# Sliding-window attention with a mixture of adapters: q and k in 16-row runs, v as fp32 with a cast on GpSimd, contiguous score columns, and a list-scheduled emission

## The chip, the cores and the metric

The kernel runs on one core of a Trainium2 chip. The metric is the time of one execution on the device in microseconds (us); lower is better. Times "before" are of the kernel as it stood, "after" of the changed one.

## The reference

```python
def _attn_ref(q, k, v):                  # q, k, v: (8, 8, 576, 64) = batch, head, position, d
    window = 32
    scores = (1.0 / np.sqrt(D)) * np.matmul(q, k.transpose(0, 1, 3, 2))
    mask = np.abs(pos[:, None] - pos[None, :]) <= window
    scores = np.where(mask, scores, -1000000000.0)
    attn = np.exp(scores - np.max(scores, axis=-1, keepdims=True))
    attn = attn / (np.sum(attn, axis=-1, keepdims=True) + 1e-09)
    return np.matmul(attn, v)

def _moe_ref(x, w_gate, A, B):           # x: (4608, 512), 8 adapters of rank 16
    logits = x @ w_gate                  # the two largest logits of a row choose two adapters
    # w = softmax over these two; delta = sum over the two of w * ((x @ A[e]) @ B[e])
    return (x + delta).astype(np.float32)

x = attn_out.transpose(0, 2, 1, 3).reshape(B * S, H * D)   # heads side by side
```

## The kernel before

**Units.** Two heads of a batch make a pair; 8 batches of 4 pairs give 32 units. A unit has 9 blocks of 64 keys; a block meets the 128 queries around it. Two heads stand in one matmul: kT holds the pair's keys as a block-diagonal 128 x 128 weight, so the 128 score rows are 64 keys of each head. The 288 blocks are taken 8 at a time: 36 score tiles.

**Stages.** `load` (L75) brings q and k of a batch with a cast to fp16, three DMAs of 96 partitions each for q and three for k, in runs of two rows (512 bytes read, 256 written). `load_v` (L86) brings v of a batch with a cast, straight into `vbd`, in 16 DMAs of 288 runs each (256 bytes read, 128 written). All of them are issued by GpSimd (POOL). `pair_heads` (L92, VectorE) puts the heads of a pair side by side, `transposes` (L167) turns them on TensorE, and `qTs`, `kTs` receive them (L171 and L176 on VectorE, L177 on ScalarE). `score` adds the mask by a matmul with the identity (L182, two of 512 columns per tile), then one matmul of 128 columns per block (L186); its result is written with a step of two columns in PSUM. ScalarE takes the exponential (L191) into one of four `PTs`. `pv` (L206) is 13 matmuls of 130 columns per unit, and VectorE normalises (L214, L215) into `xs`.

**Adapters.** Per batch `moe_step` transposes xs (L227, copied by L230), multiplies by A and w_gate (`moe_zl`, L238), runs a chain of small VectorE operations for the gate (L248 to L262, with one exponential on ScalarE, L254), transposes the result (L271, copied by ScalarE L274) and forms B's part plus xs (L282, L284), which ScalarE copies out (L287) and SP stores (L291).

**Order.** The program emits unit by unit: transposes two units ahead, scores one unit ahead, `pv` of the unit, then a quarter of the previous batch's `moe_step`. PSUM tiles come from a pool of three of 4 KB per partition (`pw`) and one of two of 2 KB (`pt`). Each engine runs its instructions in the order in which they stand. A DMA that POOL issues waits, besides what its data asks for, on the semaphore of the eighth POOL DMA before it, since eight such semaphores are used in turn; DMAs of SP have eight of their own.

**Start.** POOL issues q and k of batch 0, makes `ident`, issues v of batch 0, and makes `mask`.

Of the kernel before, what the change touches and what calls it, by code (L numbers as in the profile page):

```python
# [21 lines left out]

@with_exitstack
def kernel(
# [37 lines left out]

    NV = 3
    vbd = [const.tile([128, NP, NB, 2 * VD], F16, name=f"vbd{i}") for i in range(NV)]

    def load(b, w):
        d = load_pool.tile([96, 3, H, 2, D], F16, tag=f"l{w}", name=f"l{w}")
        src = (q, k)[w][b].rearrange("h (g p j) d -> g p h (j d)", g=3, j=2)
        for g in range(3):
            nc.gpsimd.dma_start(  # L75
                out=d[:, g].rearrange("p h j d -> p h (j d)"), in_=src[g])
        raw[b, w] = d

    def load_v(b):
        d = vbd[b % NV]  # L80
        src = v[b].rearrange("(n h) (a p j) d -> h j n p a d", h=2, p=32, j=2)
        for n in range(NP):
            for h in range(2):
                for j in range(2):
                    p0 = 64 * h + 32 * j
                    nc.gpsimd.dma_start(  # L86
                        out=d[p0:p0 + 32, n, :, VD * h:VD * h + D], in_=src[h, j, n])

    def pair_heads(b, w):
        d = cast_pool.tile([96, 3, 2, H, D], F16, tag=f"c{w}", name=f"c{w}")  # L90
        for g in range(3):
            nc.vector.tensor_copy(out=d[:, g],  # L92
                                  in_=raw[b, w][:, g].rearrange("p h j d -> p j h d"))
        qk[b, w] = d

    raw, qk = {}, {}
    load(0, 0)
    load(0, 1)

    ident = const.tile([128, 128], F16)  # L100
    make_identity(nc, ident)

    for i in range(NV):
        nc.vector.memset(vbd[i], 0.0)
        nc.vector.memset(vbd[i][0:64, :, :, D], 1.0)
        nc.vector.memset(vbd[i][64:128, :, :, VD + D], 1.0)

    load_v(0)
    pair_heads(0, 0)
    pair_heads(0, 1)  # L110


    mask = const.tile([128, 4, 128], F16)
    nc.gpsimd.memset(mask, 0.0)
    for s in range(4):
        jk = s % 2
        blk = mask[32 * s:32 * s + 32]
        nc.gpsimd.affine_select(out=blk, in_=blk, compare_op=ALU.is_ge, fill=NEG,
                                base=-jk, channel_multiplier=-2,
                                pattern=[[0, 4], [1, 128]])  # L120
        nc.gpsimd.affine_select(out=blk, in_=blk, compare_op=ALU.is_ge, fill=NEG,  # L121
                                base=64 + jk, channel_multiplier=2,
                                pattern=[[0, 4], [-1, 128]])

    NQ = 4
    qTs = [const.tile([128, 2, 320], F16, name=f"qT{i}") for i in range(NQ)]
    kTs = [const.tile([128, NB, 128], F16, name=f"kT{i}") for i in range(NQ)]
    for t in qTs:
        nc.vector.memset(t[:, :, 0:16], 0.0)
# [245 lines left out]
```

## Time and profile before

| | us |
|---|---|
| median of 2 runs | 216.5 (215.47 and 217.53) |
| span of the profiled execution | 211.4 |
| from the start to the first `pv` matmul | 34.3 |
| from there to the last `pv` | 159.5 |
| from there to the end | 17.6 |

The page gives the profiled execution by its span, from the first to the last instruction; 216.5 stands 5.1 us above it. Durations below come from this one execution. PE is TensorE's matmuls, PEld its weight loads, DVE VectorE, ACT ScalarE, POOL GpSimd, SP the engine that issues the stores. A run of matmuls is pipelined: the mean of one (some 220 ns for 128 columns) is not its price in a stream, which is read from the chain of waits, where a run of n matmuls stands with its share of the time.

### The profile page before, as it was taken

The page shows a single profiled execution, that of the slowest core. Times are in us where ns is not written, and L with a number is a line of the kernel's source. Part 1 is how long each engine was busy: PE and PEld are TensorE (multiplying, and loading weights), DVE is VectorE, ACT ScalarE, POOL GpSimd, SP SyncE. Part 2 cuts the span into 40 slices and gives each one's busy share as a digit, 9 for nine tenths or more (in the row PEclk, how much of TensorE's full clock was granted, in tenths as well). Part 3 has the DMA queues.
Part 4 walks back from the last instruction along what each step waited for, and adds up shares of the span by engine and source line. Part 5 has one row for each costly group of instructions (what it writes and reads, how often), then busy time and mean ns, then how long its engine had stood idle before and what let it go on. Part 6 is the DMA issues. An engine that isn't in the chain of part 4 may idle for free.

```text
span 211.4 us, 4124 instructions
## 1 busy us (share of the span) xinstructions
PE 147.6 (70%) x1600; PEld 114.4 (54%) x1600; DVE 119.9 (57%) x337; ACT 85.6 (40%) x109; POOL 128.3 (61%) x197
## 2 busy tenths in 40 slices
PE   0030279998299949987699729964998599848481
PEld 0010158996268835876378626864687468726330
DVE  6787026668814891379346851688349734844700
ACT  2001015663357334553275144723683466246032
POOL 7999995999799469835983797699480000000000
PEclk9999999999969995999699997999999999999955
DMA  6998099999999998998999999999993023003306
GB/s 59 157 63 56 1 140 125 67 42 154 138 101 144 244 96 54 208 210 87 63 167 249 103 89 153 258 98 147 172 189 55 0 90 136 5 0 123 100 0 223
DMA packets 86642, 24.12 MB, mean 114 GB/s; under 512 B 81888, under 2 KB 82016, under 8 KB 86624
## 3 DMA queue, kind: packets, MB, share of 16 engines
q0 software_dynamic: 81376, 14.44, 86.3%
q1 hardware_dynamic: 5248, 9.44, 13.2%
q8 instruction: 12, 0.20, 0.4%
q14 instruction: 6, 0.05, 0.1%
HBM read 28.85 MB, written 9.44 MB: 181 GB/s over the span
## 4 chain that ended last, share of the span: by engine, by line
PE 52%; DVE 19%; POOL 11%; ACT 9%; issue 4%; DMA 3%; ACTq 0%; POOLq 0%
PE ps L186 13%; PE po L206 9%; PE ps L182 7%; PE pd L282 5%; PE tp L167 5%; PE pd L284 5%; POOL vbd_82 L86 4%; DVE xb L215 4%; PE pz L238 3%; DMA l_189<-in_k_dram 3%; DVE zs L262 3%; PE tx L227 3%; DVE xT L230 3%; ACT zT L274 3%; PE tz L271 2%
## 5 line engine op out<-in xcount | busy, mean ns | idle before, releaser
L86 POOL DMA_DIRECT2D vbd_83<-in_v_dram x48 | 29.3, 616 | 12.0 <-DMA vbd_83<-in_v_dram 4.8
L86 POOL DMA_DIRECT2D vbd_82<-in_v_dram x48 | 29.3, 617 | 9.0 <-DMA l_496<-in_q_dram 2.7
L182 PE MATMUL ps<-mask,ident 128*128 128x512 f16 x72 | 24.6, 423 | 12.7 <-POOL mask L121 12.0
L214 DVE RECIPROCAL rc<-po 128x10 f32<-128x10 f32 x32 | 7.0, 218 | 38.2 <-PE po L206 38.1
L287 ACT COPY obt<-pd 128x1024 f32<-128x1024 f32 (+1 forms) x24 | 20.8, 869 | 16.8 <-PE pd L284 16.0
L215 DVE TENSOR_TENSOR xb<-po,rc 128x640 f16<-128x640 f32 x32 | 26.2, 820 | 0.7
L86 POOL DMA_DIRECT2D vbd_84<-in_v_dram x32 | 19.5, 619 | 7.3 <-DMA vbd_84<-in_v_dram 2.6
L282 PE MATMUL pd<-B_sb,zT 128*128 128x512 f16 x40 | 18.3, 459 | 4.2 <-ACT zT L274 4.2
L271 PE MATMUL tz<-ident,zs 128*128 128x128 f16 x40 | 4.0, 234 | 21.0 <-DVE zs L262 21.0
L227 PE MATMUL tx<-ident,xb 128*128 128x128 f16 x160 | 14.7, 220 | 5.4 <-DVE xT L230 4.8
L284 PE MATMUL pd<-xb,ident 128*128 128x512 f16 x40 | 18.4, 461 | 0.0
L230 DVE COPY xT<-tx 128x512 f16<-128x512 f16 x40 | 15.6, 416 | 2.4 <-PE tx L227 1.6
L177 ACT COPY kT_164<-tp 64x576 f16<-64x576 f16 x8 | 5.1, 633 | 25.0 <-DVE kT_164 L176 25.0
L227 PEld LDWEIGHTS <-xb 128*128 128x128 f16 x160 | 11.3, 101 | 6.9 <-issue 4.9
L271 PEld LDWEIGHTS <-zs 128*128 128x128 f16 x40 | 2.4, 102 | 22.8 <-DVE zs L262 22.8
L182 PEld LDWEIGHTS <-ident 128*128 128x128 f16 x72 | 6.6, 110 | 14.3 <-issue 14.1
L238 PE MATMUL pz<-WA_sb,xT 128*128 128x136 f16 x160 | 13.9, 223 | 0.4 <-DVE xT L230 0.4
L186 PE MATMUL ps<-qT_160,kT_164 128*128 128x128 f16 x72 | 11.1, 317 | 2.4 <-ACT kT_164 L177 2.4
L177 ACT COPY kT_161<-tp 64x576 f16<-64x576 f16 x8 | 5.1, 634 | 18.2 <-DVE kT_161 L176 18.1
L274 ACT COPY zT<-tz 128x640 f16<-128x640 f16 x8 | 5.5, 692 | 16.6 <-PE tz L271 16.6
L191 ACT ACTIVATE PT_178<-ps 128x1024 f16<-128x1024 f32 x9 | 9.2, 1023 | 6.6 <-PE ps L186 5.7
L191 ACT ACTIVATE PT_180<-ps 128x1024 f16<-128x1024 f32 x9 | 9.2, 1023 | 6.1 <-PE ps L186 5.2
(209 smaller groups left out, 375.4 us busy)
## 6 DMA issues: line engine op xcount, KB each, us to landing
out_dram<-obt SPq DMA_DIRECT2D x24, 256.0 KB, 4.0
out_dram<-obt SPq DMA_DIRECT2D x16, 192.0 KB, 2.7
vbd_82<-in_v_dram POOLq DMA_DIRECT2D x48, 36.0 KB, 2.8
vbd_83<-in_v_dram POOLq DMA_DIRECT2D x48, 36.0 KB, 3.4
vbd_84<-in_v_dram POOLq DMA_DIRECT2D x32, 36.0 KB, 3.2
l_85<-in_q_dram POOLq DMA_DIRECT2D x3, 192.0 KB, 4.8
l_89<-in_k_dram POOLq DMA_DIRECT2D x3, 192.0 KB, 6.4
l_185<-in_q_dram POOLq DMA_DIRECT2D x3, 192.0 KB, 4.6
```

What stands on the lines that cost most here:

```text
L86: nc.gpsimd.dma_start(out=d[p0:p0 + 32, n, :, VD * h:VD * h + D], in_=src[h, j, n])
L182: nc.tensor.matmul(out=ps[:, i:i + 4], lhsT=ident, rhs=mask, start=True, stop=False)
L186: nc.tensor.matmul(out=ps[:, i].rearrange("p (k j) -> p j k", j=2), lhsT=kTs[u % NQ][:, a, :], rhs=qTs[u % NQ][:, :, 32 * a:32 * a + 64], ...
L191: nc.scalar.activation(out=PTs[t % NPT][:, :, 64:192], in_=ps, func=AF.Exp, scale=1.0 / float(D) ** 0.5)
L206: nc.tensor.matmul(out=po[:, GS * g:GS * g + 2 * VD], lhsT=PTs[t % NPT][:, sl, off:off + 128], rhs=vbd[b % NV][:, n, a, :], start=(i == 0) ...
L215: nc.vector.tensor_tensor(out=xs[b][:, :, 128 * n:128 * n + 128].rearrange("p g (h d) -> p g h d", h=2), in0=pog[:, :, :, 0:D], in1=bcast( ...
L227: nc.tensor.matmul(out=tp[:, 128 * c:128 * c + 128], lhsT=xs[b][:, g, 128 * c:128 * c + 128], rhs=ident, is_transpose=True, start=True, st ...
L230: nc.vector.tensor_copy(out=st[b, "xT"][:, g].rearrange("p c k -> p (c k)"), in_=tp[:, 0:512])
L238: nc.tensor.matmul(out=pz[:, GS * g:GS * g + ER + E], lhsT=xT[:, g, c, :], rhs=WA_sb[:, c, :], start=(c == 0), stop=(c == 3))
L282: nc.tensor.matmul(out=pd[:, i], lhsT=zT[:, g], rhs=B_sb, start=True, stop=False)
L284: nc.tensor.matmul(out=pd[:, i], lhsT=ident, rhs=xs[b][:, g], start=False, stop=True)
L287: nc.scalar.copy(out=ob[:, 0:n], in_=pd[:, 0:n])
```

## The change

q and k are no longer loaded batch by batch. A row of a load tile is a run of 16 rows of one pair (4 KB read per head); 128 such runs make a tile, nine tiles hold all of q (and of k). VectorE regroups the heads of a tile (one copy), TensorE transposes it in 16 pieces of 128 x 128, and the pieces go into one resident `qT` and into three `kT` buffers. Queries and keys stand in a permuted order within a block, so the mask matmul takes a permuted identity (`pk`) and the output a second one (`po_`). A score matmul writes 128 neighbouring columns; its moving operand `qT` is read in runs of 4 elements (8 bytes) with a long step. v comes as fp32 on SP's queue (8 DMAs of 576 runs of 256 bytes per batch) into `vraw`, and GpSimd casts it into `vbd` by `affine_select`, one head half (64 partitions x 2304 elements) at a time. Weights come in 11 DMAs instead of 6. xs is transposed and copied two groups at a time. A planner takes every piece of work with an engine, a cost and a due time, and fixes the order of emission.

```diff
+class Planner:            # list scheduling: at each free engine the ready task with the earliest due time
+    LAT = 0.12
+            for e in engines:
...
+                for t in sorted(ready[e], key=lambda t: (t["due"], t["n"])):
+                    if all(self.slots[p] for p, _ in t["take"]):
+                        break
...
-    def load(b, w):
-        d = load_pool.tile([96, 3, H, 2, D], F16, tag=f"l{w}", name=f"l{w}")
-        src = (q, k)[w][b].rearrange("h (g p j) d -> g p h (j d)", g=3, j=2)
+    def load(t, w):
+            src = qkv[w][b].rearrange("(hh n) (s r) d -> (n s) hh (r d)", hh=2, r=RR)
+            nc.gpsimd.dma_start(out=d[i - 128 * t:e - 128 * t], in_=src[i - BI * b:e - BI * b])
...
     def load_v(b):
-        d = vbd[b % NV]
-                    nc.gpsimd.dma_start(
-                        out=d[p0:p0 + 32, n, :, VD * h:VD * h + D], in_=src[h, j, n])
+        d = vraw[slot("vr", b)].rearrange("(hh r s) a d -> hh s r a d", hh=2, s=4)
+                nc.sync.dma_start(out=d[hh, s], in_=src[hh, s])
+    P.add("ldw", "POOL", 6.5, -2, load_w, ["dq1.0"])
...
+    def cast_v(b, hh):
+        nc.gpsimd.affine_select(out=o, in_=i_, compare_op=ALU.is_ge, fill=0.0,
+                                base=1, channel_multiplier=0,
+                                pattern=[[0, NP * NB], [0, D]])
+            P.add(f"cv{b}.{hh}", "POOL", 2.9, 4 * b - 2.5 + 0.1 * hh,
...
+    def regroup(t, w):
+        s = raw[2 * slot("raw" + "qk"[w], t) + w].rearrange("p h (r d) -> p r h d", d=D)
+        nc.vector.tensor_copy(out=rg[slot("rg", (t, w))], in_=s)
+    def trans(t, w, x):
+        for r in range(8):
+            nc.tensor.matmul(out=tp[:, r], lhsT=src[:, 8 * x + r], rhs=ident,
+                             is_transpose=True, start=True, stop=True)
...
     def score(t):
         for i in range(0, TB, 4):
-            nc.tensor.matmul(out=ps[:, i:i + 4], lhsT=ident, rhs=mask,
-                             start=True, stop=False)
+            nc.tensor.matmul(out=ps[:, i:i + 4], lhsT=pk, rhs=mk, start=True, stop=False)
         for i in range(TB):
-                out=ps[:, i].rearrange("p (k j) -> p j k", j=2),
-                lhsT=kTs[u % NQ][:, a, :],
-                rhs=qTs[u % NQ][:, :, 32 * a:32 * a + 64],
+                out=ps[:, i],
+                lhsT=kT[slot("kT", g // 32)][:, g % 32].rearrange("p h c -> p (h c)"),
+                rhs=qT[:, :, c0:c0 + 8].rearrange("p r (h s) -> p h r s", h=2),
                 start=False, stop=(i % 4 == 3))
...
+        P.add(f"g1{b}", "DVE", 1.1, d0 - 1, lambda b=b: gate1(b), [f"zl{b}"]
+        P.add(f"g2{b}", "DVE", 2.1, d0 - 1, lambda b=b: gate2(b), [f"ge{b}"],
...
+    plan = P.run()
+    with tc.manual_schedule():
+        for t in plan:
+            place.update(t["held"])
+            t["emit"]()
```

POOL at the start of the program, before (l: q and k, vbd: v of batch 0):

```order
L75 DMA l_85<-in_q_dram 96x8x128 x3
L75 DMA l_89<-in_k_dram 96x8x128 x3
masks.py:197 MEMSET ident 128x128
L114 MEMSET mask 128x512
masks.py:199 ISA
masks.py:199 AFFINE_SELECT ident<-ident 128x128
L86 DMA vbd_82<-in_v_dram 32x9x64 x16
L118 AFFINE_SELECT mask<-mask 32x512 x2
```

POOL in the change, from the last load of tile 3 (raw_62: k; vraw_74: v of batch 0; DMASWn: the semaphores of POOL's DMAs):

```order
L252 DMA raw_62<-in_k_dram 80x2x1024 [waits DMASW5_49]
L215 MEMSET kT_72 128x2048 [waits Pool_49]
L289 AFFINE_SELECT vbd_76<-vraw_74 64x36x64 [waits DMAHW4_49,DMAHW6_49,DMAHW2_49,DMAHW0_49]
L266 DMA WA<-in_moe_A_dram 64x8x16 [waits DMASW6_49]
...
L266 DMA WA<-in_moe_A_dram 64x8x16 [waits DMASW5_49]
L270 DMA WA<-in_moe_w_gate_dram 64x4x8 [waits DMASW6_49]
L270 DMA WA<-in_moe_w_gate_dram 64x4x8 [waits DMASW7_49]
L271 DMA Bsb<-in_moe_B_dram 128x512 [waits DMASW0_49]
L289 AFFINE_SELECT vbd_76<-vraw_74 64x36x64 [waits DMAHW5_49,DMAHW3_49,DMAHW7_49,DMAHW1_49,Pool_49]
```

The second cast of batch 0's v, without which no `pv` can start, stands behind all 11 loads of weights, and the eighth of these waits on the semaphore of tile 3's last load.

VectorE around the gate of one batch, before (m, is, lm, dm, s, gate, zs: the gate; c: `pair_heads`):

```order
L248 TENSOR_REDUCE m_954<-pz 128x5
L171 COPY qT_160<-tp 128x2x288
L92 COPY c_827<-l_496 96x1024
L249 TENSOR_TENSOR is_958<-pz,m_954 128x40
L176 COPY kT_164<-tp 64x9x64
L250 SCALAR_TENSOR_TENSOR lm<-is_958,pz 128x40
L92 COPY c_976<-l_500 96x1024
L252 TENSOR_REDUCE m_955<-lm 128x5
L92 COPY c_976<-l_500 96x1024
L253 TENSOR_TENSOR dm<-m_955,m_954 128x5
```

and in the change:

```order
L462 TENSOR_REDUCE m_110<-W_98 128x5
L463 TENSOR_TENSOR is_118<-W_98,m_110 128x40
L464 SCALAR_TENSOR_TENSOR lm_120<-is_118,W_98 128x40
L466 TENSOR_REDUCE m_112<-lm_120 128x5
L467 TENSOR_TENSOR dm_114<-m_112,m_110 128x5
L409 RECIPROCAL rc_95<-W_99 128x10
L410 TENSOR_TENSOR xs_84<-W_99,rc_95 128x5x128
L476 TENSOR_TENSOR is_122<-lm_120,m_112 128x40
```

The copies that stood between the gate's operations are gone from there; one normalisation (L409, L410) stands between its two halves. On PE the pieces between a batch's `moe_zl` and its transposes of zs were 12 transposes, 8 score matmuls and one `pv` (13) before; in the change, for batch 1, three `pv`, three score tiles and 16 transposes.

## Rows read from the trace of the kernel before

**Rows 1.** The page: busy time by engine, PE over 40 slices, chain by engine.

```profile
PE 147.6 (70%) x1600; PEld 114.4 (54%) x1600; DVE 119.9 (57%) x337; ACT 85.6 (40%) x109; POOL 128.3 (61%) x197
...
PE   0030279998299949987699729964998599848481
...
PE 52%; DVE 19%; POOL 11%; ACT 9%; issue 4%; DMA 3%; ACTq 0%; POOLq 0%
```

**Rows 2.** Three stretches: length; busy (instructions) of PE, PEld, DVE, ACT, POOL; clock, DMA, GB/s.

```profile
0.00:34.30 34.30, 9.96 (x60) 6.96 (x61) 17.99 (x39) 4.25 (x5) 31.51 (x49) 1.00 1.00 86
34.30:193.80 159.50, 129.53 (x1490) 103.46 (x1487) 96.30 (x279) 76.95 (x99) 96.78 (x149) 0.95 1.08 121
193.80:211.40 17.60, 8.13 (x56) 3.96 (x53) 5.58 (x19) 4.36 (x7) 0.00 (x0) 0.71 0.32 108
```

**Rows 3.** Waits of PE in 34.3 to 193.8: us in total, times, longest.

```profile
PE tz L271 <- DVE zs L262: 17.9, 7, 3.3
PE tx L227 <- DVE xT L230: 4.4, 5, 1.3
PE pd L282 <- ACT zT L274: 3.4, 7, 0.7
PE ps L186 <- ACT kT_164 L177: 2.4, 3, 1.3
```

**Rows 4.** The chain of waits, pieces in order of time: start, us, what.

```profile
50.46 1.18 PE pz L238 x20
...
52.08 0.89 PE ps L186 x8
...
64.44 0.43 PE ps L182 x2
...
67.05 0.75 PE po L206 x13
...
68.23 0.51 PE tp L167 x12
...
71.19 0.45 PE tx L227 x8
...
81.76 0.43 PE pd L282
```

**Rows 5.** Timeline, gate of two batches: start, us, instruction [idle before <-releaser].

```profile
74.03 0.18 DVE L248 TENSOR_REDUCE m_954<-pz 128x5 f32<-128x40 f32 x1
...
78.34 0.82 DVE L262 TENSOR_TENSOR zs<-pz,gate 128x640 f16<-128x640 f32 x1
...
197.99 0.20 DVE L248 TENSOR_REDUCE m_2739<-pz 128x5 f32<-128x40 f32 x1 [0.51 <-PE pz L238]
...
200.12 0.82 DVE L262 TENSOR_TENSOR zs<-pz,gate 128x640 f16<-128x640 f32 x1
```

**Rows 6.** Timeline of the start.

```profile
1.29 2.42 POOL L75 DMA_DIRECT2D l_85<-in_q_dram  x3 [0.83 <-POOLq L359]
...
24.89 2.29 PE L182 MATMUL ps<-mask,ident 128*128 128x512 f16 x5 [11.99 <-POOL mask L121]
...
32.58 0.60 POOL L86 DMA_DIRECT2D vbd_83<-in_v_dram  x1 [0.65 <-DMA l_185<-in_q_dram]
```

**Rows 7.** Groups of instructions: what, count | busy us, mean ns | idle before.

```profile
L144 POOL DMA_DIRECT2D WA_sb<-in_moe_A_dram x4 | 3.5, 897 | 0.0
...
L118 POOL TENSOR_SCALAR_AFFINE_SELECT mask<-mask 32x512 f16<-32x512 f16 x4 | 2.5, 633 | 0.2
...
L92 DVE COPY c_1957<-l_1493 96x1024 f16<-96x1024 f16 x3 | 1.8, 609 | 0.0
...
L92 DVE COPY c_275<-l_185 96x1024 f16<-96x1024 f16 x3 | 1.3, 423 | 10.7 <-DMA l_185<-in_q_dram 10.7
```

**Rows 8.** DMA, 2 to 12 us: GB/s written, 40 slices; then 9 to 20 us: v's issues.

```profile
GB/s 0 0 0 15 46 78 91 154 180 175 154 162 171 167 157 107 111 131 149 148 168 163 173 164 161 164 161 177 180 176 181 174 155 143 81 71 118 49 29 100
...
vbd_82<-in_v_dram POOLq DMA_DIRECT2D x16, 36.0 KB, 2.6
```

**Rows 9.** The page: the queue of SP's DMAs, packets, MB, share of 16 engines.

```profile
q1 hardware_dynamic: 5248, 9.44, 13.2%
```

More of the change, by code (lines that the diff above doesn't have):

```diff
@@ L89, in pair_heads @@
[L89 to L123, printed above, removed]
@@ new lines @@
+    RR = 16
+    SL = S // RR
+    NI = NU * SL
+    NTI = NI // 128
+    PADQ = 2
+    QW = NI + 2 * PADQ
+    BI = NP * SL
+    const = tc.alloc_tile_pool(name="const", bufs=1)
+    psum = tc.alloc_tile_pool(name="psum", bufs=1, space=bass.MemoryType.PSUM)
+    NRAW, NRG, NKB, NVR, NVB, NPT, NX, NOB = 3, 3, 3, 2, 3, 4, 3, 3
+    raw = [const.tile([128, 2, RR * D], F16, name=f"raw{i}") for i in range(2 * NRAW)]
+    rg = [const.tile([128, RR, 2, D], F16, name=f"rg{i}") for i in range(NRG)]
+    qT = const.tile([128, RR, QW], F16, name="qT")
@@ new lines @@
+    P.add("ident", "POOL", 3.0, -8, c_ident)
+    P.add("perm", "POOL", 1.5, -6, c_perm, ["ident"])
+    P.add("mask", "POOL", 1.5, -5.5, c_mask)
+    P.add("pad", "DVE", 0.3, -10, c_pad)
+    P.add("ckT0", "DVE", 2.2, -9, lambda: c_kT(0))
+    P.add("cvb0", "DVE", 2.6, -8, lambda: c_vb(0, nc.vector))
+    for i in range(NPT):
+        P.add(f"cPT{i}", "DVE", 1.1, -7 + i, lambda i=i: c_PT(i))
+    for i in range(1, NKB):
+        P.add(f"ckT{i}", "POOL", 2.0, 2.0 * i - 3, lambda i=i: c_kT(i))
+    for i in range(1, NVB):
+        P.add(f"cvb{i}", "POOL", 2.6, 3.0 * i - 3, lambda i=i: c_vb(i, nc.gpsimd))
@@ new lines @@
+    for t in range(NTI):
+        for w in range(2):
+            P.add(f"ld{t}.{w}", "POOL", 0.8, tile_due(t) - 14 + 0.1 * w,
+                  lambda t=t, w=w: load(t, w), [], take=[("raw" + "qk"[w], t)])
+            P.add(f"dq{t}.{w}", "DMA", 2.7, tile_due(t) - 14 + 0.1 * w, None,
+                  [f"ld{t}.{w}"], lat=2.0)
+    for b in range(B):
+        P.add(f"lv{b}", "SP", 4.8, 4 * b - 14, lambda b=b: load_v(b), [], take=[("vr", b)])
+        P.add(f"dv{b}", "DMA", 4.5, 4 * b - 13, None, [f"lv{b}"], lat=2.0)
@@ L192, in score @@
                              func=AF.Exp, scale=1.0 / float(D) ** 0.5)
-    xs = {}
+    for t in range(NT):
+        b0, b1 = TB * t, TB * t + TB - 1
+        tiles = range(b0 // 32, min(NTI - 1, b1 // 32) + 1)
+        dep = []
+        for tt in tiles:
+            dep += [f"eq{tt}.{x}" for x in range(2)] + [f"ekj{tt}.{x}" for x in range(2)]
+        if (4 * b1 + 5) // 128 < NTI and (4 * b1 + 5) // 128 not in tiles:
+            dep += [f"eq{(4 * b1 + 5) // 128}.{x}" for x in range(2)]
+        drop = [("kT", b1 // 32)] if b1 % 32 == 31 else []
+        P.add(f"sc{t}", "PE", 0.92, TB * t / NB, lambda t=t: score(t),
+              dep + ["mask", "perm", "pad"], take=[("W", ("s", t)), ("PT", t)], drop=drop)
+        P.add(f"ex{t}", "ACT", 1.02, TB * t / NB, lambda t=t: expo(t), [f"sc{t}"]
+              + ([f"cPT{t}"] if t < NPT else []),
+              drop=[("W", ("s", t))])
@@ L233, in moe_zl @@
     def moe_zl(b):
[L234 to L235 removed]
+        pz = W[slot("W", ("z", b))]
         for g in range(NG):
[L237 removed]
+            for c in range(NP):
                 nc.tensor.matmul(out=pz[:, GS * g:GS * g + ER + E],
[L239 to L241 removed]
```

478 lines of the change are left out of this document (315 added, 163 removed).

## The prediction, on record before the changed kernel ran

> **What bounds the kernel now.** I read the page first. No engine is full: PE is busy 70% of the span, POOL 61%, DVE 57%, and the chain that ended last is 52% PE, 19% DVE and 11% POOL [rows 1]. PE's row over 40 slices shows three parts: almost nothing until some 30 us, a long dense part, a thin end. Three windows measure them: 34.3 us before the first `pv`, 159.5 us from there to the last one, 17.6 us after it [rows 2]. In the middle part PE works 129.5 us and waits 30. Its waits there, read by releaser, are mostly one: the transposes of zs wait 17.9 us in 7 batches for the last gate operation; behind it come the copies of xT, zT and kT [rows 3]. The DMA share is 1.08 in the middle, but PE's list of waits has no DMA in it: loads run ahead. So the middle part is bound by PE's own stream and by its order, the first part by POOL and what POOL waits for.
>
> The chain of waits gives prices of PE's work in a stream [rows 4]: a score tile is 0.43 (two mask matmuls of 512 columns) and 0.89 (eight of 128, 111 ns each); 13 `pv` matmuls of 130 columns take 0.75 (58 ns each); 12 transposes of 96 columns 0.51; eight of 128 columns 0.45 (56 ns); `moe_zl` 1.18. The score matmul, with its stepped write, costs twice what equal columns cost elsewhere.
>
> **The change part by part.** I sum against this execution's span of 211.4; the median of the runs stands 5.1 above it.
>
> *Score columns.* 32 of the 36 tiles fall in the middle part. With contiguous columns eight matmuls should take 8 x 0.058 = 0.46 instead of 0.89: 32 x 0.43 = 13.8 less. The moving operand is now read in 8-byte runs, which no row shows. Bounds: nothing gained (111 ns stays) to 13.8. A loss I exclude: 512 columns behind a wait took 0.43 for one matmul in the piece at 81.76 [rows 4], 108 ns per 128 columns, and no row is slower. The cause that the rows show is the write, since the old read was in long runs; I take **-13.3**.
>
> *Transposes.* 64 x 6 at 0.51/12 are 16.3; 288 at 56 ns are 16.1. **Nothing**.
>
> *The gate.* From its first operation to zs the chain took 5.1 us in a middle batch and 2.95 in the last one, where nothing stood between [rows 5]. The pieces on PE meanwhile were 12 transposes, 8 score matmuls and a `pv`: 0.51 + 0.89 + 0.75 = 2.15, and the rest was the wait. In the change the chain is 2.95 and one normalisation (about 1 us): 4.0. PE's cover is 2.4 us in batch 0, 4.0 to 5.9 in batches 1 to 5, 1.7 in batch 6. So about 1.6 and 2.3 us stay: 17.9 becomes 4. **-14**; bounds 0 and -17.9.
>
> *The other waits* (11.7 us, four kinds and some small ones [rows 2, 3]): q and k are transposed tiles ahead, xs in larger steps. I take half: **-6**; bounds 0 and -11.7, since three PSUM tiles and two small ones are still all there are, and new waits on them can come.
>
> *Half-paced matmuls.* Counts times stream prices give 32 x 1.32 + 32 x 0.75 + 60 x 0.255 + 7 x (1.12 + 1.18 + 0.28 + 10 x 0.215) = 115 us for the middle; PE was busy 129.5. The 14.7 between are runs' ends and matmuls that ran at half pace behind a wait (0.43 for 512 columns against 0.215). With a third of the waits left I take half: **-7**; bounds 0 and -14.7.
>
> *VectorE and ScalarE.* 48 copies at 0.42 become 18 of twice the length, 0.85 at most [rows 7]: 20 becomes 15 at most; q and k copies move the same elements. DVE's 96 us of 159.5 become some 93 of 119: hidden, but no longer loose.
>
> *POOL.* 128 v issues of 0.60 go [rows 6]; 16 casts come, each 2304 elements at L118's 633 ns per 512 [rows 7]: 2.85, 46 in all. Of these 14 lie in the middle, 40 us beside 119; with them go the DMA issues of tiles 4 to 8. Hidden.
>
> *The start.* This is what I expect to get worse. The first `pv` needs both casts of batch 0. The second stands behind 11 loads of weights, and the eighth of those waits for the eighth POOL DMA before it, the last load of tile 3. That such a wait is real the old trace shows: a v issue sat 0.65 us until an unrelated q load had landed [rows 6]. So q and k of four tiles (8.39 MB) and v of two batches (2.36 MB) must first have come. q and k arrived at up to 180 GB/s as fp16 [rows 8], 360 as read: 23.3 us. v: at the same rate 6.6; at the rate at which it came (288 runs per 0.60 issue, 121 GB/s) 19.5. With a start at 1.3 [rows 6] and 2.0 of landing (2.6 less the issue [rows 8]) the last load lands between 33 and 46. Four more issues (0.9 at most each [rows 7]) and the cast give the first `pv` at 39.6 to 52.6 against 34.3. I take 42.3, near the lower end, because v's old rate was that of its issues: **+8**; bounds +5 and +18. PE's early work (four score tiles, two tiles' transposes) is hidden in it. Mask and identity, which PE awaited 12 us before [rows 6], are no longer last.
>
> *The end* keeps its chain: **0**.
>
> Sum: 8 - 13.3 - 14 - 6 - 7 = -32.3. Span 179, first part 42, middle 119.2, end 17.6; with 5.1, **184 us**.
>
> **The lock.** While POOL issued q and k, three copies of VectorE took 609 ns on average, where the same copy took 423 at another time [rows 7]; 0.19 more each. Fifteen regroupings at that rate lose 3 us, and DVE has room. The Trainium skill (SBUF — State Buffer, "SBUF: two separate sides") says more: a VectorE operation in a two-port mode and a GpSimd operation hold the shared port pair exclusively, and the later one waits out the whole instruction of the other. By that rule a copy would wait for a cast to end; the rows show a slowing only, and no operation of POOL as long as a cast beside such a copy.
>
> **Rivals.**
> 1. *The columns stay dear.* The 8-byte reads cost as much as the stepped write did: 184 + 13.3 = 197.
> 2. *The order does not fit.* The planner's costs are guesses; where a real duration differs, engines that run in order wait. For: five of PE's waits are on other engines' copies. If the 30 us of idle time and the half pace stay, 211.4 + 8 - 13.3 + 5.1 = 211.
> 3. *A regrouping waits out a cast* (the rule above as a mechanism here). Casts fill 40 of 119 us, so a third of 15 regroupings meets one and waits half of 2.85, 7 us, with PE waiting behind: 191. For: the three slow copies; against: 0.19, not 1.4.
> 4. *v on SP's queue is paced by its packets, and the kernel gets slower.* SP's queue took 13.2% of 16 x 211.4 us for 5248 packets [rows 9]: 85 ns each, of up to 2 KB. Were that the price of a packet of any size, a batch of v (4608, 288 per engine) takes 24.5 us and eight take 196; then the last casts (5.7), three units (3.85 each) and the end: 1.3 + 196 + 5.7 + 11.6 + 17.6 + 5.1 = 237. It decides the time from 62 ns a packet, and makes it slower than before by over 2% from 78. Against it: on POOL's queue 18 runs of 256 bytes per engine went by in each 0.60 us, 34 ns or less, and landed in 2.6 without piling up [rows 8]. For: no row shows small packets on this queue.
>
> **Chances.** Forecast 0.57, rival 1 0.12, rival 2 0.13, rival 3 0.09, rival 4 0.09. The range: the forecast's own bounds (all gains full, start +5: 164; start +18: 194) rarely fall together; I cut to 167 below and reach to 209 above, which takes in rivals 1 and 3 and the late start, and leaves out rival 4 and most of rival 2. A difference within 2% (212.2 to 220.8) is about what cannot be told from no change. Faster: forecast, 1, 3 and a third of 2: 0.82. Same: most of the rest of 2: 0.08. Slower: rival 4 and a little of 2: 0.10.
>
> **What would show it.** Right: score matmuls by eights at 0.45 to 0.5 in the chain; the first `pv` at 40 to 45 us, with POOL waiting for loads of k ahead of its weights; less than 6 us of waits for zs; some 120 us from first to last `pv`; v landing within 10 us per batch. Wrong in a named way: eights at 0.9 (rival 1); PE idle 25 us or more in the middle with new releasers (2); regroupings of 2 us (3); POOL's casts waiting for v, batch after batch (4). The forecast fails too if VectorE, at nearly 80% of the middle, turns out to set the pace.

## The result, and the profile after

The changed kernel takes **193.7 us** (median of two runs, 193.4 and 194.0) against 216.5: a ratio of 0.893 with a 95% interval of 0.881 to 0.905. The prediction said 184, and 167 to 209 as a range. The profiled execution has a span of 191.6 us, 2.1 below the median (before: 5.1). Some executions of one and the same kernel take 1.5% and more longer than its fastest, at a lower granted clock; the traces of E5, E6, E9 and E10 below are of executions that took 1.8 to 2.7% more than the fastest of their kernel, and are read for shares and waits, not for a microsecond.

The page of the changed kernel: busy time by engine, PE over 40 slices, the queue of SP's DMAs, the chain by engine and by line (the rows that answer to [rows 1] and [rows 9]):

```profile
PE 129.3 (67%) x1504; PEld 101.6 (53%) x1504; DVE 118.4 (62%) x248; ACT 81.4 (42%) x95; POOL 79.5 (41%) x80
...
PE   0067620029667769997998795869699799949280
...
q1 hardware_dynamic: 43136, 18.88, 37.8%
...
PE 38%; DVE 24%; SPq 12%; issue 8%; POOL 6%; ACT 6%; DMA 3%; ACTq 1%; DVEq 0%; POOLq 0%
```

PE is busy 18 us less, the other engines about as before, except POOL (128 to 80). A new name stands in the chain: SPq, the engine that issues v. The three stretches, with the same columns as [rows 2]:

```profile
0.00:41.97 41.97, 11.08 (x120) 8.82 (x121) 17.35 (x25) 9.00 (x9) 26.82 (x41) 0.84 1.05 167
41.97:168.50 126.53, 107.26 (x1317) 87.22 (x1316) 93.80 (x198) 65.67 (x76) 52.69 (x39) 0.94 0.67 154
168.50:191.60 23.10, 10.91 (x69) 5.54 (x67) 7.29 (x26) 6.73 (x10) 0.00 (x0) 0.80 0.30 102
```

| stretch | before | predicted | after |
|---|---|---|---|
| to the first `pv` | 34.3 | 42.3 | 42.0 |
| first to last `pv` | 159.5 | 119.2 | 126.5 |
| PE busy in it | 129.5 | 109.2 | 107.3 |
| PE idle in it | 30 | 10 | 19.3 |
| from there to the end | 17.6 | 17.6 | 23.1 |
| median less span | 5.1 | 5.1 | 2.1 |

The miss of 9.7 is the middle (+7.3: idle time 9.3 more, busy time 1.9 less) and the end (+5.5), less 3 at the offset. In the runs of the kernel before that came later, a run's time stands 1.8 to 2.3 us above its own span; so some 3 of the 5.1 were not an offset, but the two runs of the median being longer than the execution that was profiled. PE's waits in the middle, to be held against [rows 3] (the first row of the view, 16.3 us for the first `pv`, ends where the stretch begins and is left out, as are rows of 1.0 us and less):

```profile
PE W L357 <- DVE xs L410: 2.5, 3, 1.4
PE T L492 <- DVE qT L315: 2.3, 3, 1.0
PE W L397 <- DVE zs L484: 2.2, 3, 0.7
PE T L436 <- ACT kT L323: 2.2, 2, 1.1
PE T L492 <- DVE zs L484: 2.1, 1, 2.1
PE T L436 <- DVE xT L441: 2.0, 2, 1.1
PE T L436 <- DVE xs L410: 2.0, 1, 2.0
PE W L357 <- ACT ob L514: 1.3, 3, 0.7
```

The 17.9 us of the transposes of zs (now L492) are 4.4, of which 2.1 are put down to zs itself; 2.2 more are waits of `pv` (L397) for the PSUM tile that zs is computed from. What is left is no longer one wait but many small ones. By what each instruction writes and reads, 14.7 of the 18.8 us of the view (all rows but the first) are waits for a PSUM tile to be read empty: xs, zs, ob and PT are read out of the three tiles W, and qT, kT and xT out of the two tiles T.

In the chain of waits (start, us, what) the score columns cost what was predicted, 0.49 instead of 0.89, and the matmul behind a wait still runs at half pace (0.85):

```profile
71.00 0.85 PE W L361 x8
...
75.47 0.49 PE W L361 x8
...
77.28 0.43 PE W L357 x2
77.71 0.49 PE W L361 x8
```

The same chain at the start (vraw: v as it lands, vbd: v after the cast):

```profile
3.57 2.19 SPq L260
5.80 6.63 SPq L260
12.48 5.06 SPq L260
17.58 6.49 SPq L260
24.12 5.83 DMA vraw<-in_v_dram
29.94 2.35 POOL vbd L289
32.29 5.14 POOL WA L266 x8
37.62 1.32 POOL WA L270 x2
38.94 0.56 POOL Bsb L271
39.56 2.37 POOL vbd L289
41.97 4.22 PE W L397 x39
```

The first four v issues, ahead of these rows, take 0.61 to 0.69 us each; then one takes up to 6.6, while q and k are loading as well (DMA share 1.05 up to the first `pv`). So what the first cast needs of v has landed at 29.9 only; after that cast the weights' issues follow one another without a gap, and the second cast ends at 41.9. The weights wait for no semaphore: the last load of tile 3 had landed at 28.8.

VectorE's regroupings (L304), and what GpSimd does beside them (timelines, start, us, instruction; last, the group of all 18):

```profile
47.21 4.91 DVE L304 COPY rg<-raw 128x2048 f16<-128x2048 f16 x2
...
53.62 1.03 DVE L304 COPY rg<-raw 128x2048 f16<-128x2048 f16 x1
```

```profile
47.01 1.81 POOL L215 MEMSET kT<- 128x2048 f32 x1
48.89 2.68 POOL L289 TENSOR_SCALAR_AFFINE_SELECT vbd<-vraw 64x2304 f16<-64x2304 f32 x1
```

```profile
L304 DVE COPY rg<-raw 128x2048 f16<-128x2048 f16 x18 | 19.5, 1099 | 0.0
```

Two copies, which take some 0.65 us when GpSimd is idle, took 2.15 and 2.84. The first ended 0.54 us after GpSimd's memset (48.82), the second 0.55 us after the cast (51.57): each stood until GpSimd's instruction was over and then took about its own time. Of the 18 regroupings five are lengthened, three by a cast and two by a memset.

### The profile page after: what moved, and what is told of

Same layout as the page of the kernel before. It is cut to its first block, busy times and chain, and to the rows that moved or that the text cites. A ratio compares the mean times of both kernels' runs of the same rounds, so it can differ in the third digit from the quotient of the medians.

```text
span 191.6 us, 3791 instructions
## 1 busy us (share of the span) xinstructions
PE 129.3 (67%) x1504; PEld 101.6 (53%) x1504; DVE 118.4 (62%) x248; ACT 81.4 (42%) x95; POOL 79.5 (41%) x80
## 3 DMA queue, kind: packets, MB, share of 16 engines
q1 hardware_dynamic: 43136, 18.88, 37.8%
## 4 chain that ended last, share of the span: by engine, by line
PE 38%; DVE 24%; SPq 12%; issue 8%; POOL 6%; ACT 6%; DMA 3%; ACTq 1%; DVEq 0%; POOLq 0%
SPq L260 12%; PE W L397 7%; PE W L449 5%; DVE xs L410 5%; PE W L357 5%; PE W L361 5%; PE W L505 5%; PE W L507 4%; PE T L310 4%; DMA vraw<-in_v_dram 3%; DVE rg L304 3%; POOL WA L266 3%; DVE kT L323 3%; DVE zs L484 3%; POOL vbd L289 2%
## 5 line engine op out<-in xcount | busy, mean ns | idle before, releaser
L368 ACT ACTIVATE PT<-W 128x1024 f16<-128x1024 f32 x36 | 35.8, 1027 | 36.7 <-PE W L361 36.5
L289 POOL TENSOR_SCALAR_AFFINE_SELECT vbd<-vraw 64x2304 f16<-64x2304 f32 x16 | 38.6, 2412 | 30.7 <-DMA vraw<-in_v_dram 21.6
L397 PE MATMUL W<-vbd,PT 128*128 128x130 f16 x416 | 29.7, 228 | 18.5 <-POOL vbd L289 16.3
L397 PEld LDWEIGHTS <-PT 128*128 128x128 f16 x416 | 27.1, 102 | 19.8 <-issue 19.5
L310 PE MATMUL T<-ident,rg 128*128 128x128 f16 x288 | 23.6, 240 | 14.8 <-DVE rg L304 13.1
L323 ACT COPY kT<-T 64x1024 f16<-64x1024 f16 x18 | 17.9, 1007 | 29.3 <-DVE kT L323 24.7
L310 PEld LDWEIGHTS <-rg 128*128 128x128 f16 x288 | 20.6, 109 | 17.7 <-DVE rg L304 13.7
L410 DVE TENSOR_TENSOR xs<-W,rc 128x640 f16<-128x640 f32 x32 | 26.4, 824 | 1.1
L514 ACT COPY ob<-W 128x1024 f32<-128x1024 f32 (+1 forms) x24 | 20.2, 871 | 13.9 <-PE W L507 13.8
L361 PEld LDWEIGHTS <-kT 128*128 128x128 f16 x288 | 20.3, 99 | 10.2 <-ACT kT L323 1.6
L357 PE MATMUL W<-mask,pk 128*128 128x512 f16 x72 | 21.9, 386 | 4.5 <-DVE xs L410 2.5
L361 PE MATMUL W<-qT,kT 128*128 128x128 f16 x288 | 23.8, 225 | 1.2 <-ACT kT L323 1.0
L409 DVE RECIPROCAL rc<-W 128x10 f32<-128x10 f32 x32 | 6.8, 213 | 27.2 <-PE W L397 27.0
L304 DVE COPY rg<-raw 128x2048 f16<-128x2048 f16 x18 | 19.5, 1099 | 0.0
L315 DVE COPY qT<-T 128x1024 f16<-128x1024 f16 x18 | 12.3, 686 | 8.0 <-PE T L310 7.2
L252 POOL DMA_DIRECT2D raw<-in_q_dram x16 | 10.9, 689 | 7.3 <-DVE rg L304 5.2
```

Source lines behind the costliest of these rows:

```text
L289: nc.gpsimd.affine_select(out=o, in_=i_, compare_op=ALU.is_ge, fill=0.0, base=1, channel_multiplier=0, pattern=[[0, NP * NB], [0, D]])
L304: nc.vector.tensor_copy(out=rg[slot("rg", (t, w))], in_=s)
L310: nc.tensor.matmul(out=tp[:, r], lhsT=src[:, 8 * x + r], rhs=ident, is_transpose=True, start=True, stop=True)
L323: eng(out=o[:, :, 8 * x:8 * x + 8], in_=tp[p0:p0 + 64])
L357: nc.tensor.matmul(out=ps[:, i:i + 4], lhsT=pk, rhs=mk, start=True, stop=False)
L361: nc.tensor.matmul(out=ps[:, i], lhsT=kT[slot("kT", g // 32)][:, g % 32].rearrange("p h c -> p (h c)"), rhs=qT[:, :, c0:c0 + 8].rearrange( ...
```

## The experiments

Times are medians of four runs (E9: ten), with the lowest and the highest; the ratio is to the kernel before, run on the same chip in turn. The changed kernel's is 0.893 (0.881 to 0.905), so a difference of about 2% between two variants is at the edge of what the times alone tell; windows of the traces then say where it lies.

| | kernel | us | ratio (95%) |
|---|---|---|---|
| E1 | weights behind both casts of batch 0 | 194.0 (193.3 to 197.0) | 0.901 (0.887 to 0.915) |
| E2 | and tiles 2 on behind them | 191.4 (189.9 to 193.7) | 0.889 (0.877 to 0.901) |
| E3 | casts in six pieces | 195.9 (193.5 to 197.0) | 0.905 (0.889 to 0.922) |
| E4 | other order at the end | 189.5 (186.8 to 190.7) | 0.875 (0.857 to 0.894) |
| E5 | other order on GpSimd | 191.4 (189.4 to 193.4) | 0.885 (0.875 to 0.895) |
| E6 | stores issued by ScalarE | 214.5 (211.0 to 215.9) | 0.984 (0.972 to 0.997) |
| E7 | stepped columns again | 198.7 (196.0 to 201.5) | 0.922 (0.912 to 0.932) |
| E8 | casts on ScalarE | 185.2 (185.0 to 187.3) | 0.862 (0.854 to 0.869) |
| E9 | kernel before, contiguous columns | 212.7 (211.0 to 214.7) | 0.995 (0.989 to 1.000) |
| E10 | changed kernel, order undone | 219.0 (213.1 to 220.3) | none given |
| E11 | combined | 181.4 (180.9 to 182.2) | 0.849 (0.843 to 0.856) |
| E12 | combined, late loads | 181.2 (180.3 to 184.0) | 0.847 (0.839 to 0.854) |

### E1 and E2: is the start worth its 8 us?

```diff
-    P.add("ldw", "POOL", 6.5, -2, load_w, ["dq1.0"])
+    P.add("ldw", "POOL", 6.5, -2, load_w, ["dq1.0", "cv0.1"])   # E1, E2
-                  lambda t=t, w=w: load(t, w), [], take=...
+                  lambda t=t, w=w: load(t, w), ["cv0.1"] if t >= 2 else [], take=...   # E2
```

In both runs the second cast of batch 0 is also no longer tied to the first in the plan.

> The changed kernel with the 11 loads of the weights moved behind the second cast of batch 0's v on GpSimd (both casts now stand directly one after the other); all else is left. My theory of the start: v of batch 0 lands at about 30 us, the first cast ends at 32.3, and only the weight issues (7.3 us) keep the second from following; then the first pv comes at 34.7 instead of 42.0 and the time falls by up to 7.3, to 186.5. Rival, by the theory in my prediction: the weights were held by the semaphore of tile 3's last load, so it is the loads of q and k that decide; the loads then land at 33 us or later all the same, and what is saved at the casts comes back as waits of the units behind it: 190 or more. Either way the middle part should show whether an earlier start is kept to the end: if the loads behind the weights come too late, it grows by what the start gives.

> As the kernel with the weights behind the second cast, and the loads of q and k from tile 2 on behind that cast too, so that v of batch 0 shares the memory with two tiles of q and k (4.2 MB read) instead of four. My theory: SP's first eight v issues were slow (up to 6.6 us each) because the q and k traffic filled the DMA engines at some 200 GB/s written; with half of it gone v of batch 0 lands near 17 to 20 us, the first pv comes at 22 to 26, and the time falls by 13 to 16, to 178 to 181, if the middle part keeps it. Rival: v's 576 short runs per DMA set the landing themselves, whatever else is loaded; then the first pv stays at 34 or later and the time at 186. Second rival: the loads that were put off are missed in the middle part (PE waits for transposes of tiles 2 to 4) and it grows by 8 us or more: 188 or more.

The first `pv` came at 35.0 and at 23.7, as the theory of v's landing said (in E2 the casts start at 18.84): v was held by the q and k traffic, and the second cast by the weights. But the time fell by nothing and by about 2: the middle grew to 134.8 and 142.5 (E1, then E2).

```profile
35.00:169.80 134.80, 111.32 (x1341) 91.04 (x1340) 92.30 (x203) 66.71 (x77) 59.25 (x50) 0.92 0.69 147
23.70:166.20 142.50, 106.90 (x1349) 86.85 (x1348) 90.07 (x204) 68.35 (x79) 61.35 (x55) 0.93 0.75 155
```

What PE waited for in E2:

```profile
PE W L397 <- POOL vbd L289: 11.9, 2, 11.7
PE W L397 <- ACT ob L514: 6.7, 1, 6.7
```

The 11.7 is `pv` of batch 1, whose second cast ended at 55.6 (57.0 in E1, 57.6 in the changed kernel), behind weights, loads and memsets in GpSimd's list. The 6.7 is an output copy that waited for a store, which stood on SP behind sixteen v issues:

```profile
80.34 21.79 SPq L260 DMA_DIRECT2D vraw<-in_v_dram  x16
102.24 3.35 SPq L521 DMA_DIRECT2D out_dram<-ob  x5
```

### E3: is it the lock?

```diff
-        nc.gpsimd.affine_select(out=o, in_=i_, ...
+        for j in range(6):                       # m = 36 // 6
+            nc.gpsimd.affine_select(out=o[:, m * j:m * j + m], in_=i_[:, m * j:m * j + m], ...
```

> The changed kernel with each cast of v cut into six instructions of a sixth of the length (about 0.4 us each). My theory of the middle part: a regrouping or another VectorE operation with two SBUF inputs waits for the GpSimd instruction that runs, up to its whole length, 2.4 us; that cost VectorE 7.4 us in its regroupings and some 4 in the small ones. With pieces of 0.4 us the longest regrouping falls from 2.8 to about 1.1 us, their sum from 19.5 to about 14, and the time by 2 to 5, to 189 to 191. Rival: these waits of VectorE are hidden behind PE's stream; the regroupings get shorter but the time stays within 1 us of 193.7. Second rival: each GpSimd instruction costs some 0.15 us more to start, the second cast of batch 0 ends later and nothing is gained: 194 to 195.

The regroupings fell from 19.5 to 13.9 us, VectorE's busy time from 118.4 to 111.1, and the time did not fall; the middle is 125.9 us, as in the changed kernel.

```profile
L307 DVE COPY rg<-raw 128x2048 f16<-128x2048 f16 x18 | 13.9, 785 | 0.0
```

The pieces cost more than the whole (3.0 us for six in a row, 4.95 in the batch where a regrouping stood among them, against 2.36). So the lock is real on VectorE, but it was not what the middle waited for here; the rival by which these waits are hidden behind PE's stream held.

### E4: the end

```diff
+        e0 = d0 if b < B - 1 else d0 - 5.5      # due times of xT, its copy, zl and the gate
-        P.add(f"g2{b}", "DVE", 2.1, d0 - 1, lambda b=b: gate2(b), [f"ge{b}"],
+        P.add(f"g2{b}", "DVE", 2.1, e0 - 1, lambda b=b: gate2(b),
+              [f"ge{b}"] + ([f"exx{B - 1}.2"] if b == B - 2 else []),
```

> The changed kernel with other due times for the last batch's adapter work: VectorE copies xT of batch 7 before it forms zs of batch 6, and PE does zl of batch 7 before B's part of batch 6. My theory of the end: two gate chains stand one behind the other after the last pv (zs of batch 6 ends at 171.7, zl of batch 7 starts at 175.5, zs of batch 7 ends at 181.2); with the second chain started before the first one's tail, zs of batch 7 ends some 3 us earlier, at 178, and the time falls by 2 to 3.5, to about 190.5 to 191.5. Rival: the end is bound by B's part, its copies and stores of batch 7, which run at half pace on PE after an idle stretch, and PE idles longer now: less than 1 us gained.

4 us by the medians, a little more than expected. The intervals of the ratios overlap, but the window shows the place. The row below begins 0.4 us behind the last `pv`; from that on it is 19.2 instead of 23.2, and the middle is 123.6.

```profile
166.10:184.90 18.80, 8.03 (x67) 4.60 (x67) 6.90 (x25) 6.53 (x10) 0.00 (x0) 0.93 0.37 126
```

zs of batch 7 is written at 173.4 instead of 180.4. PE has work between the two chains now, and its granted clock in the end is 0.93 instead of 0.80: about the same matmuls keep it busy for 8 us instead of 11. That is the part I had not counted.

### E5: GpSimd's list

```diff
-        P.add(f"ckT{i}", "POOL", 2.0, 2.0 * i - 3, ...
+        P.add(f"ckT{i}", "POOL", 2.0, -3.2, ...      # memsets first, while v of batch 0 is awaited
-        P.add(f"cvb{i}", "POOL", 2.6, 3.0 * i - 3, ...
+        P.add(f"cvb{i}", "POOL", 2.6, -3.1, ...
```

with the weights as in E1, batch 1's casts behind them, and the loads from tile 4 on behind those casts.

> The changed kernel with another order on GpSimd alone at its start: the memsets of the second and third kT and vbd buffers stand before the first cast (where GpSimd waits 10 us for v of batch 0), then both casts of batch 0, the weights, both casts of batch 1, and the loads of tile 4 after them. What the earlier runs showed: a first pv at 35 instead of 42, or at 24, gave almost nothing (194.0 and 191.4), and in all three kernels the second cast of batch 1 ended at 55.6 to 57.5, behind weights, loads and memsets in GpSimd's list; unit 4 started at 55.6 to 63.9. My theory now: it is this list that ate the early start. Then the casts of batch 1 end near 47, unit 4 starts at 50 to 54 instead of 63.9, and the time falls by 5 to 10, to 184 to 189. Rival: from there on the loads set the pace (the DMA engines are full to 120 us at some 200 GB/s written, and stores stand behind v's issues on SP's queue); then unit 16 still starts at 107 to 108, as in the changed kernel and in the one with late loads, and the time stays at 191 or more.

Batch 1's casts ended at 48.2 and unit 4 started at 50.6 instead of 63.2, as the theory said. But unit 16 started at 105.8 (107.1 in the changed kernel), and the time fell by 2 only: the rival's value. The lead over the changed kernel was 13 us at unit 4, 18 at unit 8 and 1 at unit 16. Meanwhile casts waited for v (11.5 us up to 71, 12.3 up to 97), and SP's issues are 33% of the chain:

```profile
71.45 4.78 POOL L289 TENSOR_SCALAR_AFFINE_SELECT vbd<-vraw 64x2304 f16<-64x2304 f32 x2 [11.47 <-DMA vraw<-in_v_dram]
...
97.32 5.27 POOL L289 TENSOR_SCALAR_AFFINE_SELECT vbd<-vraw 64x2304 f16<-64x2304 f32 x2 [12.26 <-DMA vraw<-in_v_dram]
```

### E6: stores on another queue

```diff
-            nc.sync.dma_start(out=out[r0 + lo:r0 + hi], in_=ob[lo:hi, i])
+            nc.scalar.dma_start(out=out[r0 + lo:r0 + hi], in_=ob[lo:hi, i])
-            P.add(f"st{b}.{j}", "SP", 0.6 * n, d0, ...
+            P.add(f"st{b}.{j}", "ACT", 0.6 * n, d0, ...
```

> The changed kernel with its 40 stores issued by ScalarE instead of SP, whose queue then holds v alone. Theory: in the changed kernel a store stands behind eight v issues that are slowed by full DMA engines (7 to 30 us for 8 to 15 of them), so an output buffer comes free late, and PE's tiles behind it; without that the middle part loses 2 to 5 us: 189 to 192. Rival: only the kernel with late loads, where PE waited 6.7 us for such a store, is hit by this; here the stores lag but nobody waits, ScalarE pays some 0.5 us per issue (20 in all, 10% of its span), and the time stays within 1 us of 193.7 or gets worse by up to 3.

Both were wrong: it cost about 20 us (214.5 by the median, 211.0 and 213.3 in its two fastest runs). SP's own list of waits names the cause:

```profile
SPq L260 <- DMA out_dram<-ob: 95.2, 15, 27.7
```

v's issues now wait for stores. The eight semaphores that were called SP's own at the start go round over the DMAs of both engines, as the listing of this kernel shows (its v issues wait for the semaphores that the stores were given); a v issue waits for the store that had the semaphore last, and so for the output copy ahead of that store on ScalarE. PE waited 43.9 us for casts in all. Whether a queue for the stores alone would help was not shown by this.

### E7 and E9: the price of the score columns

```diff
-                out=ps[:, i],
+                out=ps[:, i].rearrange("p (k j) -> p j k", j=2),    # E7
-                out=ps[:, i].rearrange("p (k j) -> p j k", j=2),
+                out=ps[:, i].rearrange("p (j k) -> p j k", j=2),    # E9
```

> The changed kernel with the score matmul's result written with a step of two columns, as before the change; the columns then stand in another order than the mask's and than pv takes them, so the output is not the reference's, but the amount of work is the same. Theory (my term for the score columns): the eight matmuls go back from 0.49 to 0.87 to 0.89, in 36 tiles; if PE is what the middle part goes by, the time grows by 11 to 14, to 205 to 208. Rival: the eights stay at 0.49 (then the step was not the cause of the old price). Second rival: PE is not what the middle part goes by; the eights get dearer, but the idle time of PE takes part of it, and the time grows by 3 to 8.

> The kernel before with one edit: the score matmul writes neighbouring columns instead of every second one, as in the change (the columns then stand in another order than the mask's and than pv takes them, so the output is not the reference's; the amount of work is the same). It prices the term of the score columns where PE was the bound. My prediction's term: the eights fall from 0.89 to 0.46 to 0.49 and 36 of them give 14 to 15 us of PE; 13.3 of it in the middle part: about 202 instead of 216. Rival: PE's waits (30 us in the middle part) take the place, since scores run ahead of other engines' copies and the gate: 208 or more. In the changed kernel the step put back cost only 5.

In E7 the groups of eight score matmuls went back to 0.87 and the middle to this:

```profile
42.30:170.00 127.70, 117.09 (x1317) 98.44 (x1316) 90.90 (x200) 66.53 (x76) 52.88 (x39) 0.96 0.66 152
```

PE is busy 9.8 us more than in the changed kernel, and idle 10.6 instead of 19.3: the stretch hardly grows. The step costs 3 us in all by the two fastest runs of E7 (196.0 and 198.1) and 5 by its median. In E9 the gain in the kernel before is 0.5%, at most 1.1%:

```profile
33.70:195.50 161.80, 126.93 (x1493) 96.17 (x1491) 97.55 (x283) 76.52 (x99) 97.19 (x150) 0.91 1.06 120
```

PE's busy time in the middle falls by 2.6 instead of 13.3, its idle time grows from 30 to 34.9, and the granted clock is 0.91 instead of 0.95: it stands at the lower of its two levels for 31 us of the stretch, against 17 before. (The clock is lower in all ten runs of E9, 0.90 to 0.91 over the whole run; in the three fastest runs of the kernel before in that series it is 0.94.) In both cases the rival with the waits held: the matmul is cheaper by what the chain said, and the time is not.

### E8: the casts on ScalarE

```diff
-        nc.gpsimd.affine_select(out=o, in_=i_, compare_op=ALU.is_ge, fill=0.0, ...
+        nc.scalar.copy(out=o, in_=i_)
-            P.add(f"cv{b}.{hh}", "POOL", 2.9, ...
+            P.add(f"cv{b}.{hh}", "ACT", 2.2, ...
```

> The changed kernel with the 16 casts of v done by ScalarE copies instead of GpSimd (some 2.1 us each by its rate for the copies of kT, 34 us more on ScalarE, which has 81 of 191). No cast then holds up a regrouping on VectorE, and no cast stands behind GpSimd's weights and memsets. Theory that GpSimd's list pins the first 60 us: the first pv starts at about 34.5, unit 4 at 50 to 55, and the time falls by 5 or more, to 188 or less. Theory of my third rival (the lock): regroupings fall to 0.63 to 0.7 each, VectorE's busy time by some 7 to 10, and this alone takes 2 to 5 off. Rival: the exponentials now stand behind 2 us copies on ScalarE, PE waits for PT, and what is won is lost: 192 or more.

8.5 less. The first `pv` comes at 38.8 (ScalarE waits 14.8 us for v with other work behind it), unit 4 at 53.6, regroupings take 700 ns on average and 12.5 in sum, and the end is shorter too:

```profile
38.80:162.50 123.70, 106.47 (x1351) 85.98 (x1348) 87.09 (x211) 97.89 (x95) 9.83 (x17) 0.96 0.67 158
162.50:182.80 20.30, 10.25 (x70) 5.36 (x70) 6.37 (x20) 6.62 (x9) 0.00 (x0) 0.79 0.35 117
```

Start, middle and end give about 3 each. How much of it is the lock and how much GpSimd's list is not told apart by this run: E3 and E5, which took away most of one and part of the other, gained nothing and 2. In this middle PE still waits once 4.0 us for an output copy and once 2.8 for a PT, both of ScalarE.

### E10: the order undone

```diff
-            for e in engines:
-                if free_at[e] > now + 1e-9:
+            for e in [None]:                     # one task at a time, over all engines,
+                if busy > now + 1e-9:            # in the order of due times
```

> The changed kernel with the list scheduling undone: the planner emits one piece of work after another by its due time, without regard to when an engine is free (as the hand-written order of before does), so that PE's rows go unit by unit again; GpSimd's and SP's lists also follow the due times. It prices the order: my prediction put 14 us on the wait for zs and 6 on the other waits. If that is right, PE's waits for zs come back (10 to 18 us) and the time is 205 to 215. Rival: the middle part goes by the loads, by GpSimd's list and by PE's slow clock, and the order is worth less than 5: 190 to 199.

In this run the planner also counts every piece of work as equally long. It is 219.0 by the median and 213.1 in its fastest run; the kernel before takes 214.7 and 212.3 in the same series. With the order undone, nothing of the gain is left (GpSimd's and SP's lists change with it, and are part of that price). Between first and last `pv` PE is idle 45.8 us:

```profile
28.60:200.00 171.40, 125.61 (x1400) 96.63 (x1399) 97.34 (x216) 73.51 (x85) 62.33 (x55) 0.89 0.60 128
```

Its waits over the whole run are headed by the old one:

```profile
PE T L495 <- DVE zs L487: 15.5, 7, 3.3
PE T L313 <- DVE rg L307: 13.0, 4, 11.1
PE W L400 <- ACT PT L371: 11.6, 6, 7.8
PE W L400 <- POOL vbd L292: 10.3, 1, 10.3
PE T L313 <- DVE qT L318: 8.6, 6, 6.4
```

### E11 and E12: combined

```diff
+        if b > 0:
+            return nc.scalar.copy(out=o, in_=i_)          # batch 0 stays on GpSimd
-        P.add(f"lv{b}", "SP", 4.8, 4 * b - 14, lambda b=b: load_v(b), [], take=...
+        P.add(f"lv{b}", "SP", 4.8, 4 * b - 14, lambda b=b: load_v(b),
+              [f"st{b - 4}.2"] if b >= 4 else [], take=...
```

with E1's weights and E4's end. E12 has E2's late loads and the weights ahead of the casts.

> The changed kernel with what the runs so far point to: batch 0's casts stay on GpSimd, directly one after the other and ahead of the weights; the casts of the other batches go to ScalarE; v of batch b is issued behind the stores of batch b - 4, so that no store waits behind it on SP; the last batch's adapter work is put ahead as in the kernel with the other end order. With all casts on ScalarE the time was 185.2, with the end alone 189.5 (4 less than the change). If the parts add up: 185 less 4 for the end and 2 to 4 for the stores and the first pv (35 instead of 38.8): 176 to 180. Rival: they overlap as the earlier start did: 182 to 185.

> As the combined kernel, and the loads of q and k from tile 2 on behind batch 0's casts, the weights ahead of them (GpSimd idles there). With late loads alone the first pv came at 23.7, and the gain was lost where batch 1's casts stood behind weights and loads on GpSimd and where PE waited 6.7 us for a store behind v's issues; both causes are gone here. Theory: the early start is kept in part, unit 4 starts at 42 to 48 and unit 16 at 95 to 103 instead of 108, and the time is 170 to 176. Rival: the loads set the pace over the first 100 us (the DMA engines are full from 2 us on in every version), unit 16 starts at 105 or later again and the time is that of the combined kernel, 177 to 185.

E11 and E12 are the best, and their times cannot be told apart. E11 is 15% below the kernel before and, by the ratios, 5% below the change:

```profile
0.00:34.90 34.90, 11.51 (x97) 8.55 (x98) 14.96 (x21) 8.31 (x8) 19.80 (x31) 0.89 1.01 190
34.90:160.00 125.10, 107.32 (x1340) 87.36 (x1339) 86.38 (x203) 96.32 (x92) 24.99 (x36) 0.95 0.74 159
160.00:180.20 20.20, 9.80 (x72) 5.30 (x69) 6.97 (x24) 6.42 (x9) 0.00 (x0) 0.85 0.35 118
```

Here the earlier first `pv` is kept to the end: 7 us at the start, 1 in the middle, 3 at the end; less than the sum of the parts (176 to 180) and a little below what its rival said (182 to 185). In E12 the first `pv` comes at 27.3, and of the 7.6 us won there 6 are lost again in a middle of 131.1. ScalarE waits for v of batch 1 (3.4) and for kT's memset (4.9) with other work behind it; unit 8 starts at 60.6, where in E11 it starts at 60.9. Then PE waits 12.8 us for one PT, up to 76.9: its exponential stands on ScalarE behind a cast of batch 3, which had waited 14.4 us, up to 73.8, for v. Seven of the eight issues of that v had taken SP from 36.5 to 70.6, while the loads that had been put off were under way. So a start that was moved by loading less first, in E2 and E12, was paid back later, and in E12, as in E5, it was v's slow issues that took part of it.

## Why the prediction was right, and where it was not

The direction and the range were right, and the largest term, the order, was about right. The sum was 9.7 too low, and one term, the start, came true by luck.

1. **The order** (-14 for zs, -6 for other waits, -7 for half-paced matmuls, -27 in all). Undone in E10, together with GpSimd's and SP's lists, it costs 20 to 25 (fastest run, median). The wait for zs is 4.4 as forecast, counted as all waits of its transposes or as all waits for zs. "I take half" of the other waits was the step that failed in the middle: they are 15 instead of 6, most of them for a PSUM tile to be read empty, on xs, qT, kT, xT and ob. The prediction had named this as the way it could fail ("three PSUM tiles and two small ones are still all there are"). PE's busy time was right within 2 us.
2. **The score columns** (-13.3). The price was right (0.49), its use was not. Taken back in the changed kernel they cost 3 to 5, put alone into the kernel before they gave 1. The step that failed is counting PE's busy time as time: in the row of before PE idled 30 of 159.5 us and ran part of its matmuls at a lower clock, and a cheaper matmul turned into more of both. The terms do not add: the columns alone give about 1, everything without the order nothing, everything with it 23.
3. **The start** (+8, first `pv` at 42.3). The number came true at 42.0 for another reason. I had the weights wait for the semaphore of tile 3's last load; that load had landed at 28.8, before them, and they waited for nothing. What was late was v (29.9), by SP's slow issues, and the weights' own issue time. And as a term of the sum it was worth nothing: E1 moved it by 7 us and the time stayed. Batch 1's casts stood behind the same list (E1, E2), and where they did not (E5) later casts waited for v. Only with casts on ScalarE (E8, E11) did an earlier start reach the end; which part of that edit does it is not told apart.
4. **The end** (0). It cost 5.5: the planner put a second gate chain behind the first. E4 took 4.0 of it back. "Keeps its chain" was said without looking at the order of the last batch, which the listing of the change shows.
5. **The lock** (rival 3, 191). The Trainium skill (SBUF — State Buffer, "SBUF: two separate sides") has a VectorE operation in a two-port mode and a GpSimd operation exclude each other, and the later one wait out the other's whole instruction. The trace agrees: five copies of 0.65 ended 0.54 to 0.55 us after the cast or memset beside them, and took up to 2.84. The sum on VectorE is 7 us, as the rival had it, but PE did not wait behind them: its list of waits in the middle has no regrouping, and E3 shortened them and gained nothing. The rival's time, 191, was near for other reasons.
6. **v on SP's queue** (rival 4). The mean packet is far below the 62 ns that would decide: 37.8% of 16 times 191.6 us over 43136 packets are 27 ns. But v did not land "within 10 us per batch" either: batch 0 was issued from 0.8 us on and landed at 30.2. Its harm is another one, which I had not seen: stores behind slow v issues (E2), and casts that wait for v (E5, E12).

What stays open: why the middle takes 124 to 128 us in the changed kernel, E4, E7, E8 and E11 alike, with PE busy 106 to 117 of it. No single wait is over 2.5 us there, but for the two of E8. That the number of PSUM tiles sets it is a guess from the list of waits; no run gave the kernel more of them or fewer. Nor does any run take back the 16-row loads or v's own queue alone, so what these two changes are worth is not known.

## What to carry to other kernels

A cheaper instruction on the busiest engine is worth its saving times the count only while that engine does not wait; where it idles a fifth of the stretch, first change the order, then price the instruction in the new order. An earlier start is a gain only if the next batches' inputs move with it: follow the same queue some batches further before counting it. And read the last batch's order in the listing as closely as the first's; two chains that overlap in the middle can stand in series at the end.

## What the runs showed of the hardware

- A DMA of 576 runs of 256 bytes takes SP some 0.65 us to issue in most cases, and up to 6.6 while q and k are loading as well (DMA share 1.05 over the first 42 us); the engine's later DMAs, stores too, stand behind it (E2).
- DMAs issued by SP and by ScalarE share one set of eight semaphores in this program; moving the stores to ScalarE's queue tied v to the stores and cost about 20 us.
- A VectorE copy of 128 x 2048 fp16 (0.65 us alone) that starts while GpSimd is at a cast or a memset ends 0.54 to 0.55 us after that instruction (five of five in the changed kernel). Cutting a cast of 64 x 2304 on GpSimd (2.36 us) into six made it 3.0, and 4.95 in the batch where a copy stood among the pieces.
- The fall of the granted clock is part of what a wait costs: after the last `pv` it was 0.80 in the changed kernel, with 12.2 us of idle time, and 0.93 in E4, with 10.8; about the same matmuls took PE 10.9 and 8.0 us.
